# Two-layer FFN behind attention: order of a feature's attention steps and weight pieces in the first chunk

## The chip, the core and the metric

The kernel runs on one core of one Trainium2 chip. The metric is the time of the whole kernel on the device, in microseconds (us). A core has five engines that work side by side, each through its own queue and strictly in order: TensorE (PE, matrix products; PEld is its weight load), VectorE (DVE), ScalarE (ACT), GpSimd (POOL) and SyncE (SP, which issues the DMAs here). An instruction waits on semaphores for what it reads; what is queued behind it on its engine waits with it.

## What is computed

Sparse attention over 4 batches, 8 heads, 576 positions of 64 features, then two feed-forward layers on 2304 tokens. Cut to what matters here:

```python
def _attn_ref(q, k, v):                    # (4, 8, 576, 64)
    scores = np.matmul(q, k.transpose(0, 1, 3, 2)) / np.sqrt(D)
    # heads 0-3: the 32 positions up to the query; heads 4-7: earlier positions of equal pos % 32
    scores = np.where(masks, scores, -1e9)
    attn = np.exp(scores - scores.max(-1))
    attn = attn / (attn.sum(-1) + 1e-9)
    return np.matmul(attn, v)

def _moe_ref(x, w_in, w_out):              # (2304, 512) -> 2048 -> 512
    h = x @ w_in
    return (h - np.tanh(h)) @ w_out

def _moe2_ref(x, w_gate, w_val, w_out):    # 512 -> 1536 -> 512
    g = x @ w_gate
    return (g / (1 + np.exp(-g)) * (x @ w_val)) @ w_out
```

## The kernel before

Products of the layers are made in three matmuls each, with high and low parts of both factors (`mm3`, L188). So weights and activations have to be split first. The weights arrive as 64-bit words, and a piece of 128 x 512 of them goes through a chain of steps, the class `Piece` (L112): `high` and `low` on ACT (L124, L127), `clamp` and `shift` on DVE (L130, L134), `join` on POOL (L142), `sign` on DVE (L146), `head` on ACT (L152, the high part), `rest` on POOL (L155, the low part). Between the steps of a piece lie a few hundred nanoseconds to some microseconds, so `Feed.tick` (L178) interleaves three pieces: one tick loads a piece two ahead of its first use, does `high`, `low` of piece t, `clamp`, `shift`, `join` of piece t-1, and `sign`, `head`, `rest` of piece t-2.

The kernel has stages: attention of the first batch (with the first four pieces), the first layer in five chunks of up to 512 tokens (L1015), and the second layer. In a chunk, f runs over 16 blocks of 128 of the hidden features: `first_part` (L513, 12 matmuls of 512 columns into `ps_h`), `bend` (L518: tanh on ACT, L520, difference on DVE, L521), `parts` (L524: high part `gh` on ACT, L527, low part `gl` on DVE, L528), and one iteration later `second` (L531, 12 matmuls into the four banks `ps_acc`). Chunk 0 is the one in which the weights are still being prepared, two ticks per iteration: 32 pieces in all, of which 28 are made here; later chunks use them again.

Into the iterations of the first chunks the attention of the following batch is threaded, one `Group` (L252) of three query blocks of a pair of heads per iteration; in chunk 0 these are 12 groups, f = 0 to 11. A group's steps: `scores` (six matmuls, PE), `top` (masked scores and their minimum after a change of sign, three instructions on DVE, L273), `exp` (three on ACT with the row sums, L282), `norm` (a small step on ACT, L290, a reciprocal on DVE, L294, and the scaling of the three blocks on POOL, L296; this is called the normalisation), `turn` (three transposes on PE, L308), `bring` (copy to SBUF on DVE, L312), `value` (six matmuls, PE) and `keep` (copy on ACT, L330).

The order of instructions in each queue is the order of these calls, written out by hand (`tc.manual_schedule`). In chunk 0 one iteration f reads, before the change: normalisation of group f-1; `first_part` of f; `bend`; look-ahead loads; `value` and `keep` of group f-3; first tick; `scores` and `top` of group f; `second` of f-1; `turn` and `bring` of group f-1; `parts` of f; `exp` of group f; second tick. The buffers: `ps_h` has two banks, `ps_a`, which scores, transposes and values share, has two, `s` has three, the staged pieces five.

Of the kernel before, what the change touches and what calls it, by code (L numbers as in the profile page):

```python
# [13 lines left out]
AF = mybir.ActivationFunctionType  # L14
ALU = mybir.AluOpType
AX = mybir.AxisListType.X
# [27 lines left out]
KC = DM // P  # L44
# [29 lines left out]
def model_kernel(ctx: ExitStack, tc: tile.TileContext, q, k, v, mask, ident, sq, sk, sv, smask, w1, w2, out):  # L74
    nc = tc.nc
# [23 lines left out]
    def psum(pool, tag):  # L99
        return pool.tile([P, 512], F32, tag=tag, name=f"ps_{tag}")  # L100
# [94 lines left out]
    with tc.manual_schedule():  # L195
# [47 lines left out]
        def load_ahead(b, s):  # L243

            i, at = divmod(s, NGRP)
            if at == (-1 if b == 0 else 0) % NGRP and (i or b == 0):
                load_qk(b, i + 1 + (b == 0))
            i, at = divmod(s - 3, NGRP)
            if at == 0 and i > 0:
                load_v(b, i + 1)  # L250

        class Group:  # L252
# [25 lines left out]
            def exp(self):  # L278
                w = self.w
                self.sm = att.tile([P, 16], F32, tag="sm", name="sm", bufs=3)[:, :GB]  # L280
                for i in range(GB):
# [2 lines left out]
                        **({"accum_out": self.sm[:, i:i + 1]} if self.b else {}),  # L284
                    )

            def norm(self, eng):
                w = self.w
                if self.b:
                    nc.scalar.activation(self.sm, self.sm, AF.Copy, bias=1e-9)  # L290
                else:
                    nc.vector.tensor_reduce(out=self.sm, in_=self.s[:, :, :w], axis=AX, op=ALU.add)
                    nc.vector.tensor_scalar(self.sm, self.sm, 1e-9, None, ALU.add)
                nc.vector.reciprocal(self.sm, self.sm)  # L294
                if eng is nc.gpsimd:
                    nc.gpsimd.tensor_tensor(  # L296
                        out=self.s[:, :, :w], in0=self.s[:, :, :w], in1=self.sm.unsqueeze(2).to_broadcast([P, GB, w]),
                        op=ALU.mult,
                    )
                    return  # L300
                for i in range(GB):
                    s, r = self.s[:, i, :w], self.sm[:, i:i + 1]
                    nc.scalar.mul(s, s, r)
# [165 lines left out]
        def used(c, use):  # L469
            tag = f"w{slot_of(*use, c)}"  # L470
            if use in stream:
                c, i = divmod(c * NS + stream.index(use) + NSS, NS)
                if 0 < c < len(CHUNKS1):
                    fetching.append((c, i))
                    return
            if c >= len(CHUNKS1) - 1:
                slots.give((wpool, tag))
# [40 lines left out]
        def bend(ps, n):  # L518
            t = epool.tile([P, CHUNK], F32, tag="e", name="t")
            nc.scalar.activation(t[:, :n], ps[:, :n], AF.Tanh)  # L520
            nc.vector.tensor_tensor(out=ps[:, :n], in0=ps[:, :n], in1=t[:, :n], op=ALU.subtract)  # L521
            return ps

        def parts(t, n):  # L524
            gh = gpool.tile([P, CHUNK], F32R, tag="gh", name="gh")
            gl = gpool.tile([P, CHUNK], F32R, tag="gl", name="gl")
            nc.scalar.copy(gh[:, :n], t[:, :n])  # L527
            nc.vector.tensor_tensor(out=gl[:, :n], in0=t[:, :n], in1=gh[:, :n].bitcast(F32), op=ALU.subtract)  # L528
            return gh, gl

        def second(w, g, n, acc, start, stop):  # L531
            gh, gl = g
            for m in range(KC):
                mm3(acc[m][:, :n], w, m * P, gh[:, :n], gl[:, :n], start, stop)
# [480 lines left out]
        for c, (c0, n) in enumerate(CHUNKS1):  # L1015
# [9 lines left out]
            g = {}  # L1025
            for f in range(NF1):
                if f - 2 in gs and not strided and c > 0:
                    gs[f - 2].bring(nc.vector)
                if f - 1 in gs and not strided:
                    gs[f - 1].norm(nc.gpsimd)  # L1030
                restore()
                if strided:
                    if f == NF1 - 3 and b + 1 < B:
                        later = begin(b + 1)
                    if f == START[NGRP - 1] + 1:
                        load_qk(b, 3)
                    if f == START[NGRP - 1] + 4:
                        load_v(b, 3)
                if ahead:
                    ps = ahead.pop(0)  # L1040
                    first_part(ps, w1_t[f, 0], x, n, PAIRS[3:], False, True)
                else:
                    ps = psum(ps_h, "h")
                    first_part(ps, w1_t[f, 0], x, n, order, True, True)
                used(c, (f, 0))
                if c == last:
                    flow.run(KC * 3 * MM)
                    for eng in "AVAV":
                        flow.load(eng, 0.65)
                if c == 0 and f == 2:  # L1050
                    second(w1_t[0, 1], g.pop(0), n, acc, True, False)
                    gs[0].turn(ps_a, "a")
                t = bend(ps, n)
                if c == 0 and f == 2:
                    gs[0].bring(nc.vector)
                if c == 0:
                    load_ahead(b, f)
                if f - 3 in gs:
                    gs[f - 3].value(ps_a, "a")
                    gs[f - 3].keep()  # L1060
                if f - 2 in gs and strided:
                    gs[f - 2].bring(nc.scalar)
                if c == 0:
                    feed1.tick()
                if f in gs:
                    gs[f].scores(ps_a, "a")
                    gs[f].top()
                if f == (0 if c == 0 else 1):
                    acc = [psum(ps_acc, "acc") for _ in range(KC)]
                if c == 0 and f > 1:  # L1070
                    second(w1_t[f - 1, 1], g.pop(f - 1), n, acc, False, False)
                    used(c, (f - 1, 1))
                    if f - 1 in gs:
                        gs[f - 1].turn(ps_a, "a")
                        gs[f - 1].bring(nc.vector)
                g[f] = parts(t, n)
                if f == 0 and c > 0:
                    kept()
                if f in gs:
                    gs[f].exp()  # L1080
                if c == 0:
                    feed1.tick()
                if f > 0 and c > 0:
                    second(w1_t[f - 1, 1], g.pop(f - 1), n, acc, f == 1, False)
                    used(c, (f - 1, 1))
                    if c == last:
                        flow.run(KC * 3 * MM)
                if f - 1 in gs and c > 0:
                    gs[f - 1].turn(ps_a, "a")
                if strided:  # L1090
                    if f in gs:
                        gs[f].norm(nc.scalar)
                    strided.step(f)
                if strided and f == NF1 - 1:
                    for j in ((0, 4), (4, 8), (8, 9)):
                        strided.turn(*j, ps_a, "a")
# [362 lines left out]
```

## Time and profile before

| | |
|---|---|
| median of 3 runs | 921.43 us (920.67 to 923.9) |
| profiled execution, its own time | 920.19 us |
| its span, first to last instruction | 918.3 us |
| PE busy | 880.8 us (96%) |
| DVE busy | 644.5 us (70%) |
| ACT busy | 458.7 us (50%) |
| POOL busy | 337.5 us (37%) |
| mean granted clock of PE, share of 2.4 GHz | 0.994 |

The profile is that of one execution. Busy shares are over the whole span; chunk 0 of the first layer, which the change touches, lies between about 46 and 165 us. A wait is put down to the instruction that released it last. In a timeline a row's idle time, in brackets, is that of its own engine just before it; of the releaser named there, "POOL w L155" ahead of a POOL instruction means only that POOL was busy with that one before. Rows of one engine can overlap by some tens of nanoseconds, since an instruction starts while the one before drains.

### The profile page before, as it was taken

The numbers are of one execution on the slowest core, as the hardware profiler recorded it, in microseconds if no ns is written. First come the engines' busy times: TensorE is split into PE (matmuls) and PEld (weight loads), VectorE is DVE, ScalarE is ACT, GpSimd is POOL, SyncE is SP. The second block draws the span as 40 slices with busy tenths as digits, with TensorE's granted clock in tenths as the row PEclk, the third lists the DMA queues.
The fourth block names the chain that finished last, engine by engine and source line by source line (L and its number), as shares of the span: only waits on it lengthen the run. The fifth ranks groups of instructions, "written<-read, shape, count | busy, mean of one in ns | idle before, by whom it ended". The sixth has DMA issues, their size and how long they took to land. (4 is left out here: it accounts for less than half of the span.)

```text
span 918.3 us, 14160 instructions
## 1 busy us (share of the span) xinstructions
PE 880.8 (96%) x4918; PEld 722.3 (79%) x4918; DVE 644.5 (70%) x1222; ACT 458.7 (50%) x1034; POOL 337.5 (37%) x284
## 2 busy tenths in 40 slices
PE   8889998899999999999999988999999999999998
PEld 6567776777877778998887776888888887888888
DVE  6778786677776787326886785788877777966451
ACT  5577775534244523225555454555545446655431
POOL 2578887385526553001503421535544320000000
PEclk9899999999999999999999999999999999999999
DMA  8464743632343210426636642535452568968551
GB/s 272 154 195 155 255 158 113 241 110 82 103 140 118 69 46 24 146 85 237 221 92 205 207 149 82 183 117 165 154 184 87 200 216 291 344 229 278 198 202 42
DMA packets 66215, 150.38 MB, mean 164 GB/s; under 512 B 7200, under 2 KB 13344, under 8 KB 66144
## 3 DMA queue, kind: packets, MB, share of 16 engines
q1 hardware_dynamic: 65568, 149.04, 48.3%
q8 instruction: 39, 0.64, 0.3%
q10 hardware_dynamic: 576, 0.43, 0.2%
q14 instruction: 32, 0.26, 0.1%
HBM read 105.93 MB, written 43.52 MB: 163 GB/s over the span
## 5 line engine op out<-in xcount | busy, mean ns | idle before, releaser
L193 PE MATMUL ps_acc<-sl 128*128 128x512 f32 (+1 forms) x336 | 126.7, 377 | 5.0 <-DVE sl L738 5.0
L191 PE MATMUL ps_acc<-sl 128*128 128x512 f32 (+1 forms) x336 | 126.8, 377 | 3.4 <-ACT t L1206 3.4
L191 PE MATMUL ps_acc<-gl,w 128*128 128x512 f32 (+1 forms) x320 | 123.2, 385 | 3.4 <-DVE gl L528 3.3
L192 PE MATMUL ps_acc<-sl 128*128 128x512 f32 (+1 forms) x336 | 126.4, 376 | 0.0
L191 PE MATMUL ps_h<-xl,w 128*128 128x512 f32 (+1 forms) x320 | 121.1, 379 | 1.9 <-DVE gl L528 1.9
L193 PE MATMUL ps_h<-xh,w 128*128 128x512 f32 (+1 forms) x320 | 118.5, 370 | 0.7 <-POOL w L155 0.7
L193 PE MATMUL ps_acc<-gh,w 128*128 128x512 f32 (+1 forms) x320 | 118.5, 370 | 0.0
L192 PE MATMUL ps_acc<-gh,w 128*128 128x512 f32 (+1 forms) x320 | 118.3, 370 | 0.0
L192 PE MATMUL ps_h<-xh,w 128*128 128x512 f32 (+1 forms) x320 | 118.1, 369 | 0.0
L142 POOL TENSOR_TENSOR sl<-sl,st 128x512 int32<-128x512 int32 x36 | 52.0, 1450 | 164.6 <-DVE sl L134 134.2
L520 ACT ACTIVATE t<-ps_h 128x512 f32<-128x512 f32 (+1 forms) x80 | 44.0, 550 | 110.9 <-PE ps_h L193 110.9
L521 DVE TENSOR_TENSOR ps_h<-ps_h,t 128x512 f32<-128x512 f32 (+1 forms) x80 | 51.5, 643 | 65.5 <-ACT t L520 65.1
L976 DVE TENSOR_TENSOR sl<-sl 128x512 fp32r<-128x512 f32 (+1 forms) x120 | 73.9, 669 | 28.5 <-ACT sl L972 27.8
L528 DVE TENSOR_TENSOR gl<-ps_h,gh 128x512 fp32r<-128x512 f32 (+1 forms) x80 | 51.1, 638 | 39.5 <-ACT gh L527 38.0
L972 ACT CAST sl<-sl 128x512 fp32r<-128x512 f32 (+1 forms) x120 | 65.7, 599 | 25.2 <-DMA sl<-gd 19.0
L193 PEld LDWEIGHTS ps_acc<-sl 128*128 128x128 f32 x336 | 63.7, 190 | 17.2 <-DVE sl L738 5.9
L191 PEld LDWEIGHTS ps_acc<-sl 128*128 128x128 f32 x336 | 63.7, 190 | 16.8 <-ACT t L1206 5.5
L191 PEld LDWEIGHTS ps_acc<-gl,w 128*128 128x128 f32 x320 | 60.3, 188 | 18.5 <-DVE gl L528 6.0
L386 POOL TENSOR_TENSOR pr<-skv,sq 128x576 f32<-128x576 f32 (+8 forms) x40 | 56.3, 1437 | 50.2 <-DVE sc L393 30.6
L191 PE MATMUL ps_a<-sl 128*128 128x512 f32 (+1 forms) x192 | 70.3, 366 | 2.7 <-DVE t L1167 2.7
L192 PEld LDWEIGHTS ps_acc<-sl 128*128 128x128 f32 x336 | 63.6, 189 | 11.2
L193 PEld LDWEIGHTS ps_h<-xh,w 128*128 128x128 f32 x320 | 60.5, 189 | 11.8 <-POOL w L155 1.5
(125 smaller groups left out, 1960.9 us busy)
## 6 DMA issues: line engine op xcount, KB each, us to landing
st<-in_w SPq DMA_DIRECT2D x68, 512.0 KB, 4.7
gd<-t SPq DMA_DIRECT2D x84, 256.0 KB, 2.1
sl<-gd SPq DMA_DIRECT2D x84, 256.0 KB, 4.5
w<-w1s SPq DMA_DIRECT2D x32, 512.0 KB, 3.5
w3s<-sl SPq DMA_DIRECT2D x24, 256.0 KB, 4.0
sl<-w3s SPq DMA_DIRECT2D x24, 256.0 KB, 5.4
x2d<-o SPq DMA_DIRECT2D x18, 256.0 KB, 3.2
out_t<-t SPq DMA_DIRECT2D x18, 256.0 KB, 2.1
```

The source lines that it names most:

```text
L142: nc.gpsimd.tensor_tensor(out=mi, in0=mi, in1=self.lo, op=ALU.add)
L191: nc.tensor.matmul(ps, lhsT=wh, rhs=xl, start=start, stop=False, skip_group_check=goes_on)
L192: nc.tensor.matmul(ps, lhsT=wh, rhs=xh, start=False, stop=False, skip_group_check=goes_on)
L193: nc.tensor.matmul(ps, lhsT=wl, rhs=xh, start=False, stop=stop, skip_group_check=goes_on)
L386: nc.gpsimd.tensor_tensor(out=t, in0=x, in1=y, op=ALU.mult)
L520: nc.scalar.activation(t[:, :n], ps[:, :n], AF.Tanh)
L521: nc.vector.tensor_tensor(out=ps[:, :n], in0=ps[:, :n], in1=t[:, :n], op=ALU.subtract)
L528: nc.vector.tensor_tensor(out=gl[:, :n], in0=t[:, :n], in1=gh[:, :n].bitcast(F32), op=ALU.subtract)
L972: nc.scalar.copy(got[0][:, 0, :n], got[0][:, 1, :n].bitcast(F32))
L976: nc.vector.tensor_tensor(out=w[:, 1, :n], in0=w[:, 1, :n].bitcast(F32), in1=w[:, 0, :n].bitcast(F32), op=ALU.subtract)
```

## The change

In chunk 0 alone (c == 0) the iteration is written out anew. `norm` is cut into `least` (ACT), `invert` (DVE) and `scale` (POOL), so that they can stand apart. The new order of iteration f: `first_part`; (f = 2: `second` and `turn` of group 0 as before); `bend`; look-ahead loads; `value` and `keep` of f-3; `scores` and `top` of f; `parts` of f; `exp` and `least` of f; first tick; `second` of f-1, `turn` and `bring` of f-1; `invert` and `scale` of f; second tick. The number and the kind of instructions stay the same, and the chunks behind keep their order.

```diff
--- before.py
+++ after.py
@@ -284,14 +284,23 @@
                         **({"accum_out": self.sm[:, i:i + 1]} if self.b else {}),
                     )
 
+            def least(self):
+                nc.scalar.activation(self.sm, self.sm, AF.Copy, bias=1e-9)
+
+            def invert(self):
+                nc.vector.reciprocal(self.sm, self.sm)
+
             def norm(self, eng):
+                if self.b:
+                    self.least()
+                else:
+                    nc.vector.tensor_reduce(out=self.sm, in_=self.s[:, :, :self.w], axis=AX, op=ALU.add)
+                    nc.vector.tensor_scalar(self.sm, self.sm, 1e-9, None, ALU.add)
+                self.invert()
+                self.scale(eng)
+
+            def scale(self, eng):
                 w = self.w
-                if self.b:
-                    nc.scalar.activation(self.sm, self.sm, AF.Copy, bias=1e-9)
-                else:
-                    nc.vector.tensor_reduce(out=self.sm, in_=self.s[:, :, :w], axis=AX, op=ALU.add)
-                    nc.vector.tensor_scalar(self.sm, self.sm, 1e-9, None, ALU.add)
-                nc.vector.reciprocal(self.sm, self.sm)
                 if eng is nc.gpsimd:
                     nc.gpsimd.tensor_tensor(
                         out=self.s[:, :, :w], in0=self.s[:, :, :w], in1=self.sm.unsqueeze(2).to_broadcast([P, GB, w]),
@@ -1026,7 +1035,7 @@
             for f in range(NF1):
                 if f - 2 in gs and not strided and c > 0:
                     gs[f - 2].bring(nc.vector)
-                if f - 1 in gs and not strided:
+                if f - 1 in gs and not strided and c > 0:
                     gs[f - 1].norm(nc.gpsimd)
                 restore()
                 if strided:
@@ -1047,45 +1056,60 @@
                     flow.run(KC * 3 * MM)
                     for eng in "AVAV":
                         flow.load(eng, 0.65)
-                if c == 0 and f == 2:
-                    second(w1_t[0, 1], g.pop(0), n, acc, True, False)
-                    gs[0].turn(ps_a, "a")
+                if c == 0:
+                    if f == 0:
+                        acc = [psum(ps_acc, "acc") for _ in range(KC)]
+                    if f == 2:
+                        second(w1_t[0, 1], g.pop(0), n, acc, True, False)
+                        gs[0].turn(ps_a, "a")
+                    t = bend(ps, n)
+                    if f == 2:
+                        gs[0].bring(nc.vector)
+                    load_ahead(b, f)
+                    if f - 3 in gs:
+                        gs[f - 3].value(ps_a, "a")
+                        gs[f - 3].keep()
+                    if f in gs:
+                        gs[f].scores(ps_a, "a")
+                        gs[f].top()
+                    g[f] = parts(t, n)
+                    if f in gs:
+                        gs[f].exp()
+                        gs[f].least()
+                    feed1.tick()
+                    if f > 1:
+                        second(w1_t[f - 1, 1], g.pop(f - 1), n, acc, False, False)
+                        used(c, (f - 1, 1))
+                        if f - 1 in gs:
+                            gs[f - 1].turn(ps_a, "a")
+                            gs[f - 1].bring(nc.vector)
+                    if f in gs:
+                        gs[f].invert()
+                        gs[f].scale(nc.gpsimd)
+                    feed1.tick()
+                    continue
                 t = bend(ps, n)
-                if c == 0 and f == 2:
-                    gs[0].bring(nc.vector)
-                if c == 0:
-                    load_ahead(b, f)
                 if f - 3 in gs:
                     gs[f - 3].value(ps_a, "a")
                     gs[f - 3].keep()
                 if f - 2 in gs and strided:
                     gs[f - 2].bring(nc.scalar)
-                if c == 0:
-                    feed1.tick()
                 if f in gs:
                     gs[f].scores(ps_a, "a")
                     gs[f].top()
-                if f == (0 if c == 0 else 1):
+                if f == 1:
                     acc = [psum(ps_acc, "acc") for _ in range(KC)]
-                if c == 0 and f > 1:
-                    second(w1_t[f - 1, 1], g.pop(f - 1), n, acc, False, False)
-                    used(c, (f - 1, 1))
-                    if f - 1 in gs:
-                        gs[f - 1].turn(ps_a, "a")
-                        gs[f - 1].bring(nc.vector)
                 g[f] = parts(t, n)
-                if f == 0 and c > 0:
+                if f == 0:
                     kept()
                 if f in gs:
                     gs[f].exp()
-                if c == 0:
-                    feed1.tick()
-                if f > 0 and c > 0:
+                if f > 0:
                     second(w1_t[f - 1, 1], g.pop(f - 1), n, acc, f == 1, False)
                     used(c, (f - 1, 1))
                     if c == last:
                         flow.run(KC * 3 * MM)
-                if f - 1 in gs and c > 0:
+                if f - 1 in gs:
                     gs[f - 1].turn(ps_a, "a")
                 if strided:
                     if f in gs:
```

## Rows read from the trace of the kernel before

**Rows 1.** The page's list of engines: busy us, share of the span, instructions

```profile
PE 880.8 (96%) x4918; PEld 722.3 (79%) x4918; DVE 644.5 (70%) x1222; ACT 458.7 (50%) x1034; POOL 337.5 (37%) x284
```

**Rows 2.** PE's waits, 26 to 160 us: us in total, times, longest

```profile
PE ps_a L308 <- POOL s L296: 7.4, 11, 1.5
```

**Rows 3.** One iteration; busy (count) of PE, PEld, DVE, ACT, POOL; PEclk

```profile
81.80:89.60 7.80, 7.27 (x52) 5.48 (x51) 6.43 (x16) 5.83 (x18) 6.50 (x6) 1.00 0.41 134
```

**Rows 4.** Timeline of ACT, one iteration: start, duration, line, operation [idle before]

```profile
81.77 0.58 ACT L520 ACTIVATE t<-ps_h 128x512 f32<-128x512 f32 x1
...
85.18 0.62 ACT L152 CAST w<-m 128x512 fp32r<-128x512 f32 x1 [1.49 <-DVE m L146]
85.71 0.58 ACT L527 CAST gh<-ps_h 128x512 fp32r<-128x512 f32 x1
...
88.96 0.62 ACT L152 CAST w<-m 128x512 fp32r<-128x512 f32 x1 [0.48 <-DVE m L146]
...
89.59 0.58 ACT L520 ACTIVATE t<-ps_h 128x512 f32<-128x512 f32 x1
```

**Rows 5.** Timeline of DVE, the same iteration

```profile
81.90 0.17 DVE L294 RECIPROCAL sm<-sm 128x3 f32<-128x3 f32 x1 [0.79 <-ACT sm L290]
82.38 0.70 DVE L521 TENSOR_TENSOR ps_h<-ps_h,t 128x512 f32<-128x512 f32 x1 [0.31 <-ACT t L520]
82.99 0.83 DVE L130 TENSOR_SCALAR m<-m 128x512 f32<-128x512 f32 x1
83.86 0.69 DVE L134 TENSOR_SCALAR m<-m 128x512 int32<-128x512 int32 x1
84.47 0.68 DVE L146 SCALAR_TENSOR_TENSOR m<-st,m 128x512 int32<-128x512 int32 x1
...
85.55 0.54 DVE L312 COPY pt<-ps_a 80x384 f32<-80x384 f32 x1
86.32 0.69 DVE L528 TENSOR_TENSOR gl<-ps_h,gh 128x512 fp32r<-128x512 f32 x1 [0.22 <-ACT gh L527]
86.93 0.94 DVE L130 TENSOR_SCALAR m<-m 128x512 f32<-128x512 f32 x1
```

**Rows 6.** Timeline of POOL, the same iteration

```profile
82.23 1.30 POOL L155 TENSOR_TENSOR w<-m,w 128x512 fp32r<-128x512 f32 x1
83.50 0.77 POOL L296 TENSOR_TENSOR s<-s,sm 128x240 f32<-128x240 f32 x1
84.68 1.65 POOL L142 TENSOR_TENSOR m<-m,st 128x512 int32<-128x512 int32 x1 [0.42 <-POOL s L296]
86.28 1.30 POOL L155 TENSOR_TENSOR w<-m,w 128x512 fp32r<-128x512 f32 x1
```

**Rows 7.** Timeline of DVE, a stretch in which POOL is idle

```profile
49.66 0.42 DVE L130 TENSOR_SCALAR m<-m 128x512 f32<-128x512 f32 x1
50.11 0.43 DVE L134 TENSOR_SCALAR m<-m 128x512 int32<-128x512 int32 x1
```

**Rows 8.** Timeline of POOL near the chunk's end

```profile
156.87 1.27 POOL L155 TENSOR_TENSOR w<-m,w 128x512 fp32r<-128x512 f32 x1
```

**Rows 9.** Timeline of DVE at the same place

```profile
157.53 1.16 DVE L146 SCALAR_TENSOR_TENSOR m<-st,m 128x512 int32<-128x512 int32 x1
159.87 0.70 DVE L521 TENSOR_TENSOR ps_h<-ps_h,t 128x512 f32<-128x512 f32 x1 [1.18 <-ACT t L520]
```

**Rows 10.** Timeline of ACT, single rows of chunk 0

```profile
51.18 0.57 ACT L520 ACTIVATE t<-ps_h 128x512 f32<-128x512 f32 x1
...
58.30 0.58 ACT L520 ACTIVATE t<-ps_h 128x512 f32<-128x512 f32 x1
...
137.21 0.58 ACT L520 ACTIVATE t<-ps_h 128x512 f32<-128x512 f32 x1
...
159.25 0.59 ACT L520 ACTIVATE t<-ps_h 128x512 f32<-128x512 f32 x1
...
160.61 0.58 ACT L527 CAST gh<-ps_h 128x512 fp32r<-128x512 f32 x1 [0.77 <-DVE ps_h L521]
```

## The prediction

> **What bounds the kernel now.** I read the page's list of engines first: TensorE (PE) is busy 880.8 us of 918.3 [rows 1], so at first sight a microsecond that PE stops waiting is a microsecond off the time. Then the list of PE's waits in the stretch that the change touches, the first chunk of the first layer (46 to 165 us): 11 of its transposes wait for the normalisation on POOL, 7.4 us in all, 0.67 each [rows 2]. They are the waits that the change aims at. Third, one iteration of that chunk by engine: in 7.80 us PE is busy 7.27, DVE 6.43, ACT 5.83, POOL 6.50, at a granted clock of 1.00 (the 2.4 GHz level) [rows 3]. No engine but PE looks full. Last, the same iteration one engine at a time, and here the reading turns. Two tanh follow each other at 81.77 and 89.59 us [rows 4]. If PE set this distance, the tanh would wait for PE; ACT has no idle time before it, it has just come from the head of a weight piece at 88.96 (and a 0.1 us step). Going back from there, each step starts as the one before allows, between ACT and DVE alone: tanh 81.77, difference 82.38, clamp 82.99, shift 83.86, sign 84.47 [rows 5], head 85.18, high part 85.71 [rows 4], low part 86.32, clamp 86.93 [rows 5], a second shift and sign, head 88.96 [rows 4]. This loop is 7.82 us long and holds no PE. PE's 0.5 us of waiting in a period is what the loop leaves over, so the question is how long the loop is after the change.
>
> **What in the loop belongs to POOL.** The clamp of 82.99 takes 0.83 us and ends 0.29 after POOL's rest that ran from 82.23 for 1.30; the shift of 83.86 takes 0.69 and ends 0.28 after the normalisation (83.50, 0.77); the clamp of 86.93 takes 0.94 and ends 0.29 after the rest of 86.28 [rows 5, 6]. With POOL idle the same clamp takes 0.42 and the same shift 0.43 [rows 7]. So they wait for POOL's running instruction to end, and then need 0.28. Sign does so too: begun 0.66 after a rest that ran from 156.87 for 1.27, it took 1.16 and ended 0.55 after it [rows 8, 9]. In the other direction POOL waits for them: the join of 84.68 ends 1.18 after the sign that ended at 85.15, the normalisation 0.45 after the clamp that ended at 83.82 [rows 5, 6]. Steps that touch PSUM don't take part: the copy of 85.55 ran its 0.54 inside the join of 84.68, the low part its 0.69 inside the rest of 86.28, and neither did the reciprocal of 81.90 (0.17) [rows 5, 6].
>
> Who goes first when both wait is seen too: at 83.53 the clamp had waited and the normalisation was just ready; the clamp went first, then the normalisation, and the shift behind it [rows 5, 6]. They alternate, the one that was ready earlier first.
>
> **The change, step by step.** Nothing is computed less or more; only the order in the queues changes, in the 16 iterations of chunk 0. Removed from the head of an iteration: small ACT step, reciprocal and normalisation of the group before. Moved ahead of the first tick: scores, minimum, split, exponentials. Moved behind it: the reciprocal and the normalisation, now of this group. The two ticks, which stood half an iteration apart, now stand together with the transposed copy, the reciprocal and the normalisation between them. Queues passed: POOL's becomes join, rest, normalisation, join, rest; SP's keeps its order (look-ahead loads, then one load per tick), and its loads come two ticks ahead of use, as before; what they land in costs nothing while that holds.
>
> I walk one iteration with its tanh at 0. Difference 0.61 [rows 4, 5]. High part 0.74 behind it, 1.35 (159.87 to 160.61 [rows 9, 10]); the three minima, which ran between the sign's end at 85.15 and the copy at 85.55 [rows 5], fit in that gap. Low part 0.61 later, 1.96; first clamp 2.57 [rows 4, 5]. POOL is idle there (checked below), so clamp and shift end at 2.99 and 3.45 [rows 7], and the sign runs 3.36 to 4.05. The join, ready at 3.58, has to wait for that sign and ends 1.18 after it, at 5.23. ACT needs 2.77 from the start of the high part to the end of the exponentials and of the tick's first two steps (85.71 to 88.48, where its idle 0.48 begins [rows 4]), so with the small step its head starts at 4.2 and ends at 4.8, ahead of the join's end. DVE goes on with the copy (0.54, PE has long transposed) and the reciprocal (0.17) and reaches the second clamp near 4.6. The join runs: the clamp ends at 5.23 + 0.28 = 5.51. The rest, ready since 5.2, comes next: 5.51 + 1.17 = 6.68 (its 1.30 less the 0.13 that passes before it asks). The second shift: 6.96. The normalisation, waiting: 7.41. The second sign: 7.41 + 0.55 = 7.96. Its head starts 0.03 later and the next tanh 0.53 behind that (85.18 to 85.71 [rows 4]): 8.52. Join and rest end the list at 9.1 and 10.4, which is 1.9 in the next period, ahead of the clamp at 2.57: the pattern closes. **The period goes from 7.8 to 8.5.** What the old order had, a tick's clamp to sign beside idle POOL and its join and rest beside PSUM work of DVE, is given up in the second tick: there the loop runs through join, rest and normalisation one after the other.
>
> PE in that period: 7.27 us of work [rows 3] fit. Instead of 0.5 us PE now waits some 1.2 us per iteration, and I expect it ahead of the second product, for the rest of its weight piece, which ends at 6.7 where it ended near 5.8 (86.28 + 1.30, from the tanh of 81.77 [rows 4, 6]). The product is half of the large matmuls, under half of 7.27 us and more than a third, so the transpose behind it stands near 9.5, about 2 behind its normalisation: the 11 waits of [rows 2] vanish.
>
> The sum, iteration by iteration:
> - First one: ACT stands idle from the tanh's end (0.58) to 1.35, where the old order put two steps of a piece: +0.8.
> - Second one: 7.12 before (51.18 to 58.30 [rows 10]), where the queues were still half filled; full afterwards: 8.5, so +1.4.
> - Ten full ones: 78.91 before (58.30 to 137.21 [rows 10]). After: 85.2 plus some 0.5, as the last six groups are wider and the first has a copy more (the 0.5 is an estimate, a tenth of a normalisation's 0.77 six times): +6.8.
> - Three without attention: 22.04 before (137.21 to 159.25 [rows 10]). The walk without normalisation gives 8.07 twice; in the last, where the second tick has only its sign, 7.6: +1.7.
> - The last iteration has no tick; from its tanh on all stays as it was, and PE's wait for the last low part moves along.
>
> Together +10.7 us. The chunks behind are bound by PE with hardly a wait, and all their transfers are issued relative to this work, so nothing gives it back. The profiled execution took 920.19 (span 918.3): 930.9. The median is 921.43, 1.24 above it: 932.
>
> Bounds of what the rows don't show. The one grant that decides most is sign against normalisation after the second shift: the sign comes within 0.1 us of the shift's end, while the normalisation has waited. Should the sign win, the period is 8.52 − 0.45 = 8.07, ten times, and the sum 6.2. I take the other, by the row of 83.50 against 83.86, where the one ready earlier won. The Trainium skill has a rule on this: by "SBUF — State Buffer", section "SBUF: two separate sides", whichever of the two engines starts first gets the shared ports for its whole instruction and the other fully blocks. By it the normalisation wins and the sum is that of the walk; it does not say who is next when both wait, so it only lowers the chance of the other grant. Upwards: 0.3 us more per period, for semaphore delays in a chain that changes engine more often, gives +3.
>
> **Rivals.**
> (1) PE is the bound and the wait is simply removed: 7.4 us less [rows 2], 914. For it: 96% busy [rows 1]. It needs a loop under 7.27 us; without any waiting for POOL the walk would be 4.6 + 0.45 (49.66 to 50.11 [rows 7]) + 0.35 + 0.71 + 0.53, about 6.6. So it decides itself on whether the second tick's clamp, shift and sign wait together less than 0.6 us (and no slower than before up to 1.2); the walk has 1.9. Also if DVE kept the ports through all three, the loop would be under PE's 7.27 too. Against it: every contended row shown. The Trainium skill speaks for it: "Perfetto Trace Analysis", section "Identifying the Most-Contended Engine", says to optimise the engine with the highest occupancy first, and its next section to find the gaps on it and make what they wait for start sooner. By that the time would be 914. The trace disagrees in this stretch: ACT, at 5.83 of 7.80 us, has no idle time before the tanh.
> (2) The sign gets the ports ahead of the normalisation: +6.2, 927.6.
> (3) The delay is taken up at the chunk's end or by a transfer that was late anyway: no difference, 921.
>
> **How the numbers follow.** A comparison of this kernel can tell about 0.3% (2.8 us) from no change. The forecast has 0.76, (2) 0.11, both slower; (1) 0.08, faster; (3) 0.05. The range reaches from 926.5, one below (2), to 935.5, the forecast plus 3 and a little; (1) and (3) are left out, 0.13.
>
> **What would show it.** Right: no more waits of the transposes for the normalisation; 10 periods of 8.5 between tanh; second shifts of about 1.4 us and second signs of 1.1; new PE waits on the rest ahead of the second product. Shifts and signs that stay at 0.43 and 0.69 in the second tick prove the walk wrong, and then (1) holds. A period of 8.1 with signs of 0.7 is (2).

## The result

The changed kernel takes 935.21 us in the median, the kernel before 922.05 beside it: 1.0139 times as long (95% interval 1.0123 to 1.0156), 12.8 us more. One of its four executions took 1737.26 us; it counts in the median and not in the ratio, and nothing on record says why. The forecast was 932.0, in a range from 926.5 to 935.5. The profiled execution took 935.01 (span 933.1), 14.8 more than that of before.

The page of the changed kernel, its list of engines, beside [rows 1]:

```profile
PE 892.1 (96%) x4918; PEld 724.1 (78%) x4918; DVE 654.9 (70%) x1222; ACT 461.1 (49%) x1034; POOL 340.6 (36%) x284
```

The three largest of PE's waits in chunk 0 of the changed kernel (total us, times, longest), beside [rows 2]; its lines are nine higher behind `norm`, so 317 is the transpose, 305 the scaling, 339 `keep`:

```profile
PE ps_acc L193 <- POOL w L155: 8.8, 13, 1.1
PE ps_a L317 <- ACT x L339: 1.7, 8, 0.3
PE ps_acc L191 <- ACT w L152: 1.1, 2, 0.9
```

No transpose waits for the normalisation any more. The 7.4 us of [rows 2] are gone, and PE waits 8.8 us for the rest of weight pieces instead.

Why it waits, in one iteration. ACT of the changed kernel (start, duration, line, operation), beside [rows 4]:

```profile
86.52 0.59 ACT L529 ACTIVATE t<-ps_h 128x512 f32<-128x512 f32 x1
...
94.46 0.62 ACT L152 CAST w<-m 128x512 fp32r<-128x512 f32 x1 [1.95 <-DVE m L146]
94.99 0.59 ACT L529 ACTIVATE t<-ps_h 128x512 f32<-128x512 f32 x1
```

From tanh to tanh 8.47 us, where it was 7.82. ACT has now nothing to do for 1.95 us ahead of the second head; it waits for the sign on DVE. DVE in the same iteration, beside [rows 5]:

```profile
89.10 0.42 DVE L130 TENSOR_SCALAR m<-m 128x512 f32<-128x512 f32 x1
89.55 0.43 DVE L134 TENSOR_SCALAR m<-m 128x512 int32<-128x512 int32 x1
89.89 0.68 DVE L146 SCALAR_TENSOR_TENSOR m<-st,m 128x512 int32<-128x512 int32 x1
90.50 0.55 DVE L321 COPY pt<-ps_a 80x384 f32<-80x384 f32 x1
90.96 0.16 DVE L291 RECIPROCAL sm<-sm 128x3 f32<-128x3 f32 x1
91.05 0.97 DVE L130 TENSOR_SCALAR m<-m 128x512 f32<-128x512 f32 x1
92.05 1.39 DVE L134 TENSOR_SCALAR m<-m 128x512 int32<-128x512 int32 x1
93.36 1.07 DVE L146 SCALAR_TENSOR_TENSOR m<-st,m 128x512 int32<-128x512 int32 x1
```

and POOL, beside [rows 6]:

```profile
90.11 1.62 POOL L142 TENSOR_TENSOR m<-m,st 128x512 int32<-128x512 int32 x1 [1.75 <-issue]
91.70 1.46 POOL L155 TENSOR_TENSOR w<-m,w 128x512 fp32r<-128x512 f32 x1
93.12 0.77 POOL L305 TENSOR_TENSOR s<-s,sm 128x240 f32<-128x240 f32 x1
93.85 1.75 POOL L142 TENSOR_TENSOR m<-m,st 128x512 int32<-128x512 int32 x1
```

The first tick finds POOL idle: clamp 0.42, shift 0.43, sign 0.68, as in [rows 7]. The second runs against it: the clamp ends 0.29 us after the join (91.73), the shift 0.28 after the rest (93.16), the sign 0.54 after the normalisation (93.89). The three take 3.43 us, those of the first tick 1.53. The loop gets longer inside DVE rows that look like long instructions; a list of waits shows nothing of it.

The stretch from the first tanh of chunk 0 to the last is 112.42 us before (46.83 to 159.25 [rows 10]) and 123.07 after, 10.65 more. Single rows of ACT's timeline, first in the kernel before, then in the changed one:

```profile
46.83 0.59 ACT L520 ACTIVATE t<-ps_h 128x512 f32<-128x512 f32 x1
```

```profile
47.06 0.60 ACT L529 ACTIVATE t<-ps_h 128x512 f32<-128x512 f32 x1 [0.60 <-PE ps_h L193]
52.41 0.58 ACT L529 ACTIVATE t<-ps_h 128x512 f32<-128x512 f32 x1
60.86 0.59 ACT L529 ACTIVATE t<-ps_h 128x512 f32<-128x512 f32 x1
146.42 0.59 ACT L529 ACTIVATE t<-ps_h 128x512 f32<-128x512 f32 x1
170.13 0.59 ACT L529 ACTIVATE t<-ps_h 128x512 f32<-128x512 f32 x1
```

Of the profile's 14.8 us 0.2 lie ahead of this stretch and 3.9 behind it. Whether those 3.9 belong to the change is the question of the last experiment.

### The profile page after: what moved, and what is told of

Read it like the earlier page. It is cut to its first block, busy times and chain, and to the rows that moved or that the text cites. A ratio compares the mean times of both kernels' runs of the same rounds, so it can differ in the third digit from the quotient of the medians.

```text
span 933.1 us, 14160 instructions
## 1 busy us (share of the span) xinstructions
PE 892.1 (96%) x4918; PEld 724.1 (78%) x4918; DVE 654.9 (70%) x1222; ACT 461.1 (49%) x1034; POOL 340.6 (36%) x284
## 5 line engine op out<-in xcount | busy, mean ns | idle before, releaser
L193 PEld LDWEIGHTS ps_acc<-gh,w 128*128 128x128 f32 x320 | 60.6, 189 | 24.7 <-POOL w L155 14.4
L193 PEld LDWEIGHTS ps_acc<-sl 128*128 128x128 f32 x336 | 64.2, 191 | 17.7 <-DVE sl L747 6.3
L191 PEld LDWEIGHTS ps_acc<-sl 128*128 128x128 f32 x336 | 64.1, 191 | 17.3 <-ACT t L1230 6.0
L536 ACT CAST gh<-ps_h 128x512 fp32r<-128x512 f32 (+1 forms) x80 | 43.6, 544 | 60.1 <-DVE ps_h L530 60.1
```

The costliest lines, as they stand in the source:

```text
L191: nc.tensor.matmul(ps, lhsT=wh, rhs=xl, start=start, stop=False, skip_group_check=goes_on)
L193: nc.tensor.matmul(ps, lhsT=wl, rhs=xh, start=False, stop=stop, skip_group_check=goes_on)
```

## Experiments

Theory A is that of the prediction: DVE's clamp, shift and sign and POOL's instructions exclude each other, so chunk 0 is a loop through ACT, DVE and POOL, and its length depends on what POOL runs when these three steps come. Theory B: PE is the bound. Theory C: the cost comes from the steps moved ahead of the first tick. Each kernel's stretch from first to last tanh of chunk 0 is read from ACT's timeline of its profile and set against the 112.42 us of before; the whole time is compared with the kernel before, run beside it on the same chip. Each stretch is that of one execution; two profiles of the changed kernel differ by 0.4 us in it (123.07 and 122.66).

| kernel | chunk 0, first to last tanh | against 112.42 | usual period | whole time, ratio to before (95%) |
|---|---|---|---|---|
| before | 112.42 | | 7.79 to 7.91 | |
| changed | 123.07 | +10.65 | 8.47 to 8.59 | 1.0139 (1.0123 to 1.0156) |
| normalisation last | 118.50 | +6.1 | 8.10 to 8.11 | 1.0047 (1.0030 to 1.0063) |
| ticks apart | 116.31 | +3.9 | 8.01 to 8.16 | 1.0038 (1.0021 to 1.0056) |
| both of these | 112.77 | +0.35 | 7.80 to 7.90 | 0.9989 (0.9977 to 1.0002) |
| before, ticks together | 134.88 | +22.5 | 9.56 to 9.67 | 1.0239 (1.0214 to 1.0265) |
| before, transposes later | 113.53 | +1.1 | 7.83 to 7.95 | 1.0020 (1.0002 to 1.0037) |
| own order, scaling on POOL | 110.40 | -2.0 | 7.52 to 7.62 | 0.9964 (0.9947 to 0.9981) |
| own order, scaling on ACT | 111.55 | -0.9 | 7.25 to 7.31 | 1.0000 (0.9983 to 1.0016) |
| scaling on POOL, loads behind | 108.49 | -3.9 | 7.52 to 7.62 | 0.9968 (0.9951 to 0.9985) |
| scaling on ACT, loads behind | 108.46 | -4.0 | 7.25 to 7.33 | 0.9952 (0.9936 to 0.9968) |

The usual period leaves out one to three of the ten full periods in most kernels, also in the kernel before, which has one of 8.20. Where they bear on the argument they are named below.

### The normalisation behind the second tick

```diff
-                    if f in gs:
-                        gs[f].invert()
-                        gs[f].scale(nc.gpsimd)
                     feed1.tick()
+                    if f in gs:
+                        gs[f].invert()
+                        gs[f].scale(nc.gpsimd)
                     continue
```

> The changed kernel with one thing moved: reciprocal and normalisation stand behind the second tick, no longer between the two. Theory A (DVE's clamp, shift and sign and POOL's instructions exclude each other, and with the two ticks side by side the second one waits for join, rest and normalisation in turn): the second sign follows its shift at once and takes about 0.69, the period falls by one normalisation, from 8.5 to about 8.1 us, and the last tanh of chunk 0 comes 5 to 6.5 us later than in the kernel before instead of 10.9. The transposes wait for the normalisation again, and that costs nothing. Rival B (the stretch is bound by PE; what costs is who makes PE wait): the waits of the transposes are back, so the period is no shorter than 8.5. Rival C (the steps moved ahead of the first tick cost, the ticks don't matter): 8.5, no difference.

DVE's second tick in this kernel:

```profile
90.72 1.08 DVE L130 TENSOR_SCALAR m<-m 128x512 f32<-128x512 f32 x1
91.83 1.39 DVE L134 TENSOR_SCALAR m<-m 128x512 int32<-128x512 int32 x1
93.14 0.68 DVE L146 SCALAR_TENSOR_TENSOR m<-st,m 128x512 int32<-128x512 int32 x1
```

POOL's join and rest beside it:

```profile
89.87 1.64 POOL L142 TENSOR_TENSOR m<-m,st 128x512 int32<-128x512 int32 x1 [1.19 <-issue]
91.47 1.46 POOL L155 TENSOR_TENSOR w<-m,w 128x512 fp32r<-128x512 f32 x1
```

and the largest of PE's waits in chunk 0:

```profile
PE ps_a L317 <- POOL s L305: 8.4, 10, 1.4
```

The sign takes 0.68 again, clamp and shift still end 0.29 us after join and rest, and the period is 8.1: one normalisation of 0.45 less than the 8.52 of the walk. Ten transposes wait for the normalisation again, 8.4 us, more than the 7.4 of the kernel before, and the kernel is 0.9% faster than the changed one all the same. B and C fall here: the waits that the change took away are back and the time is shorter, and the early exponentials are still early.

### The first tick back in its place

```diff
                         gs[f - 3].keep()
+                    feed1.tick()
                     if f in gs:
                         gs[f].scores(ps_a, "a")
...
                         gs[f].least()
-                    feed1.tick()
```

> The changed kernel with one thing moved back: the first tick stands ahead of scores and minimum, half an iteration from the second; the normalisation stays ahead of the second tick. Theory A: the join and rest of the first tick run beside DVE's work on PSUM again; the second tick still has the normalisation in its way. Period about 8.05, in the three iterations without attention 7.5 as before, the last tanh 2 to 4 us later than before. Theory B: no transpose waits for the normalisation, so the time is 7 us under that of before, 914. Rival C: as the changed kernel, 8.5, since the steps moved ahead stay there.

No transpose waits for the normalisation here, as in the changed kernel, and yet it takes longer than the kernel before. DVE's second tick now:

```profile
89.76 0.40 DVE L130 TENSOR_SCALAR m<-m 128x512 f32<-128x512 f32 x1
90.19 0.69 DVE L134 TENSOR_SCALAR m<-m 128x512 int32<-128x512 int32 x1
90.80 0.68 DVE L146 SCALAR_TENSOR_TENSOR m<-st,m 128x512 int32<-128x512 int32 x1
```

Only the shift waits, for the normalisation, and ends 0.28 us after it:

```profile
89.99 0.61 POOL L305 TENSOR_TENSOR s<-s,sm 128x240 f32<-128x240 f32 x1 [0.37 <-DVE sm L291]
```

Four of the ten full periods are 8.01 to 8.04 and five, towards the wider groups, 8.15 or 8.16; one is 9.38, in which ACT waited 2.6 us for a weight piece to land. That is 1.2 us over its neighbours and belongs to no theory; such a wait stands in the kernel before as well, and comes up again below.

### Both together

> Both edits together: first tick back in its old place, reciprocal and normalisation behind the second tick. What is left of the change is that split and exponentials stand ahead of the second product. Theory A: period 7.8 and the time of the kernel before within 1 us in chunk 0. Rival C: 8.5 or thereabouts, since minimum, split and exponentials are still early.

112.77 us against 112.42, and a ratio whose interval holds 1: within that, the early split and exponentials are worth nothing and cost nothing. With the two kernels above this divides the loss of 10.65: the two ticks side by side with the normalisation last cost 5.7 (118.50 less 112.77), the normalisation ahead of the second tick alone 3.5 (116.31 less 112.77), both 10.3. Both kernels of the second difference have a late piece, with periods of 9.38 and 8.56, so about 0.5 of the 3.5 is not the order's. The two parts add up to 9.2; some 1 us comes only where both stand together.

### The kernel before with its ticks together

```diff
-                if c == 0:
-                    feed1.tick()
                 if f in gs:
                     gs[f].scores(ps_a, "a")
...
                 if c == 0:
                     feed1.tick()
+                    feed1.tick()
```

> The kernel before with one thing moved: the first tick stands directly ahead of the second, at the end of the iteration; the normalisation stays at the head of the next one. Theory A: this is the worst place, DVE's two ticks run against join, rest, join, rest and behind them the normalisation; working the queues through with the durations of the trace gives a period of 9.6 us and about 20 to 23 us in all. Theories B and C: at most some 2 us, since nothing but the weight pieces has moved, and those are used an iteration later.

22.5 us more in chunk 0, from moving steps that nobody needs before the next iteration. DVE's second tick in this kernel, and POOL at the same time:

```profile
98.86 1.52 DVE L130 TENSOR_SCALAR m<-m 128x512 f32<-128x512 f32 x1
100.42 1.39 DVE L134 TENSOR_SCALAR m<-m 128x512 int32<-128x512 int32 x1
101.73 0.68 DVE L146 SCALAR_TENSOR_TENSOR m<-st,m 128x512 int32<-128x512 int32 x1
```

```profile
98.48 1.62 POOL L142 TENSOR_TENSOR m<-m,st 128x512 int32<-128x512 int32 x1 [2.70 <-issue]
100.06 1.46 POOL L155 TENSOR_TENSOR w<-m,w 128x512 fp32r<-128x512 f32 x1
101.94 1.64 POOL L142 TENSOR_TENSOR m<-m,st 128x512 int32<-128x512 int32 x1 [0.42 <-POOL w L155]
```

The clamp ends 0.28 after the join of 98.48, the shift 0.29 after the rest of 100.06. POOL, which had to run its work in the same place, is idle 2.70 us ahead of it. This is the strongest point for A: the forecast of 20 to 23 was worked out from durations of the trace, and B and C had at most some 2.

### The kernel before without PE's wait

```diff
+                if c == 0 and f - 2 in gs:
+                    gs[f - 2].turn(ps_a, "a")
                 t = bend(ps, n)
-                if c == 0 and f == 2:
-                    gs[0].bring(nc.vector)
+                if c == 0 and f - 2 in gs:
+                    gs[f - 2].bring(nc.vector)
...
                     used(c, (f - 1, 1))
-                    if f - 1 in gs:
-                        gs[f - 1].turn(ps_a, "a")
-                        gs[f - 1].bring(nc.vector)
```

> The kernel before with one thing moved: the transposes of a group (and the copy behind them) stand 12 matmuls later in PE's queue, behind the next first product; the normalisation stays where it was. This takes the wait for the normalisation away from PE and leaves the order of the ticks alone. Theory B (PE is the bound, the 11 waits are worth their 7.4 us): the transposes no longer wait and the time falls by about 7 us. Theory A (the loop of ACT, DVE and POOL is the bound): the waits go all the same, but the time doesn't fall; the copy now stands between difference and clamp, so the period is 7.8 to 8.1 us and the time equal to 2.5 us longer.

PE's waits in chunk 0 of this kernel, the longest in total:

```profile
PE ps_a L265 <- ACT x L330: 8.5, 9, 3.4
```

The 11 waits for the normalisation are gone, and nine waits of the scores for a bank of `ps_a` have come, 8.5 us in all. The time did not fall by 7 us, it rose by 0.2%. By itself this does not decide between A and B, since PE's waits did not get less in all; it shows, as A has it, that PE's 0.5 us to spare in a period [rows 3] come back elsewhere when they are taken away in one place. One of the nine waits is 3.4 us long. In the iteration behind it PE ran partly at half clock (granted 0.81 in the mean from 68.23 to 77.01 us), that period took 8.78 us, and the tanh at its end waited 0.85 us for PE; this is most of the 1.1 us more in chunk 0.

### An order made from the theory

If A holds, an order can be worked out from the durations that keeps DVE's three steps clear of POOL's work. `at` is the number of the first tick; `step` does one step of the piece named, or nothing where it was made earlier:

```python
# scaling on ACT; f - 3, scores, minimum as before, then:
feed1.load(at + 3); feed1.do(at, "high", "low")
step(at - 1, "rebase"); step(at - 2, "sign")          # clamp, shift, sign
g[f] = parts(t, n)
gs[f].exp(); gs[f].least()
step(at - 1, "join"); step(at - 2, "head")
second(w1_t[f - 1, 1], ...); gs[f - 1].turn(ps_a, "a")
gs[f].invert(); gs[f].scale(nc.scalar)
step(at - 2, "rest")
step(at, "rebase"); step(at - 1, "sign"); step(at, "join")
feed1.load(at + 4); feed1.do(at + 1, "high", "low")
gs[f - 1].bring(nc.vector)
step(at - 1, "head"); step(at - 1, "rest")
```

The order with the scaling on POOL is, in the same words: first tick's `high`, `low`, `rebase`, `join`, `sign`; `value` and `keep`; scores and minimum; `parts`; `head`; `rebase` of the second tick; second product and transposes; `rest`; `high`, `low`, `join`, `sign` of the second tick; exponentials; `head`, `rest`; copy, reciprocal, scaling.

> An order of its own for chunk 0, made from theory A: every step of DVE that needs the port of POOL is put where POOL has just ended, with work of DVE on PSUM (minimum, low part, copy) between them; the exponentials stand behind the first half of the second tick, the normalisation on POOL last. Theory A, working the queues through with the durations of the trace: period 7.58, the three iterations without attention 7.24 each, 3 us less than before in all. Theory B: the normalisation is last in POOL's queue, so the transposes wait as before and nothing is gained.

> An order of its own for chunk 0 with the normalisation's scaling on ACT (three instructions of about 0.36 us) instead of POOL, which takes it off the port that DVE and POOL share. Theory A: the loop is then no longer than PE's own work, period 7.25 us, 4 to 5 us less than before. Rival: ACT has 5.8 us of work in a period and 1.1 more makes it the bound; then the period stays at 7.8 or above.

Most periods came out as worked out, 7.52 to 7.62 and 7.25 to 7.31; iteration 7 did not, with 9.49 in the one and 10.56 in the other. There, with the scaling on ACT:

```profile
103.02 0.66 ACT L124 ACTIVATE m<-st 128x512 f32<-128x512 f32 x1 [3.54 <-DMA st<-in_w]
```

So the theory of the loop held, and the sum did not (2.0 and 0.9 us less in chunk 0, where 3 and 4 to 5 were forecast in all): it had no term for a piece that lands late. Two more periods of the order with the scaling on ACT are long: the first, 7.70, whose cause was not followed up, and the one behind iteration 7, 8.31. In the last one PE had waited 3.30 us for a copy on DVE, late like the rest of that iteration, then ran partly at half clock (granted 0.79 in the mean from 109.25 to 117.56 us), and the tanh at its end waited 0.92 us for PE. SP's queue shows where the late piece comes from:

```profile
93.29 0.33 SPq L468 DMA_DIRECT2D w1s<-w  x1
93.67 0.42 SPq L231 DMA_DIRECT2D kt<-in_k  x1
94.14 0.78 SPq L232 DMA_DIRECT2D qt<-in_q  x1
94.98 0.48 SPq L240 DMA_DIRECT2D vt<-in_v  x1
95.58 2.91 SPq L118 DMA_DIRECT2D st<-in_w  x3
```

The piece is issued at 95.58, behind a store that waits for its rest and behind the loads of keys, queries and values, and lands 7.4 us later. The kernel before has the same order in SP's queue, and there ACT waits for the piece behind these loads too:

```profile
100.48 0.68 ACT L124 ACTIVATE m<-st 128x512 f32<-128x512 f32 x1 [2.28 <-DMA st<-in_w]
```

It was issued at 93.66 us and landed 6.7 us later, and this is the period of 8.20. In the slower loop of the changed kernel the piece is in time or nearly so: no such wait in its first profile, 0.5 us in its second.

### The look-ahead loads behind the pieces

```diff
                     t = bend(ps, n)
...
-                    load_ahead(b, f)
...
+                    load_ahead(b, f)
                     continue
```

> The order with the scaling on ACT, and one more edit: the look-ahead loads of keys, queries and values stand behind the iteration's two loads of weight pieces in SP's queue, no longer ahead of them. In the run without this edit the period was 7.26 us as worked out, but for one of 10.56 and one of 8.31, where ACT waited 3.5 us for a weight piece to land. Theory: the late piece was queued behind the three look-ahead loads (about 1 MB); with the edit that wait goes, all ten periods are about 7.3, and chunk 0 is 4 to 5 us shorter than before, the time near 918. Rival: the loads share the DMA engines and not the order is at fault, the piece lands as late as before and the time stays at 922.

> The same edit on the order with the scaling on POOL, where one period of ten was 9.50 for the same wait instead of 7.57. Theory: all ten periods about 7.6, chunk 0 some 3.5 to 4 us shorter than before, the time near 918.5. Rival: the late landing stays, and so does the time of 919.

SP's queue of the kernel with the scaling on ACT, and all that ACT waits for pieces in chunk 0:

```profile
91.93 0.33 SPq L468 DMA_DIRECT2D w1s<-w  x1
92.35 1.31 SPq L118 DMA_DIRECT2D st<-in_w  x2
93.75 0.47 SPq L231 DMA_DIRECT2D kt<-in_k  x1
```

```profile
ACT m L124 <- DMA st<-in_w: 0.4, 2, 0.3
```

The wait went from 3.7 us in this chunk to 0.4, and the kernel is faster than the one before and than the changed one: 0.9952 times the one before (0.9936 to 0.9968), where the changed one is at 1.0139. The first of its ten full periods is again 7.70, and one is still 8.26. PE, which had been busy for only 4.93 of the 7.60 us from 59.6 to 67.2, ran partly at half clock in it (0.79 granted in the mean from 67.3 to 75.5 us), and the tanh at its end waited 0.91 us for PE. At a period of 7.25 PE has next to nothing to spare: it is busy for 7.20 of the 7.20 us from 90.1 to 97.3.

```profile
67.30:75.50 8.20, 8.20 (x41) 6.30 (x43) 6.46 (x16) 6.68 (x20) 6.56 (x6) 0.79 0.43 142
```

With the scaling on POOL chunk 0 is 3.9 us shorter than before, as expected; the whole time, 0.9968, differs from that of the order without this edit (0.9964) by nothing that can be measured.

### What lies outside chunk 0

> The changed kernel itself, more often, beside the kernel before on one chip, for the part of its loss that lies outside chunk 0. Chunk 0 accounts for 10.7 us in the profile; the comparison gave 12.8 (11.3 to 14.4) and the profile 14.8, with two stretches of half clock in the second layer, behind waits of PE that the kernel before has as well. Theory: that rest comes and goes with the granted clock from run to run, as it does for the kernel before (its runs of higher mean clock are the shorter ones); then more runs bring the difference to 10.7 within 1.5, and the runs of one mean clock differ by about 10.7. Rival: the later start puts the second layer in a worse place for good, then the difference stays at 13 and the mean clock of the changed kernel is lower than that of the kernel before in the mean over the runs.

1.0113 (1.0085 to 1.0141): 10.4 us, with the 12.8 of the first comparison just inside the interval and the rival's 13 at its edge. Chunk 0 was 122.66 us in this profile, +10.2. Over the six executions of the changed kernel the mean granted clock goes from 0.988 to 0.994; the three at 0.988 took 934.69 to 937.45 us, the one at 0.994 930.48. Over the eleven of the kernel before it goes from 0.989 to 0.994; the three at 0.989 took 924.62 to 925.78, the one at 0.994 920.21. The relation is loose: the longest of the eleven, 926.36, had 0.991, and two at 0.993 differ by 2.5 us. At 0.994 the two kernels differ by 10.3 us, at 0.993 by 11.0 (933.54 against a mean of 922.5), at 0.992 by 11.9 (935.19 against a mean of 923.3). The place in the profile is the beginning of the second layer. The same 35 us in the changed kernel's first profile, in its second, and in that of before (the third number from the end of a line is PE's granted clock, ahead of DMA share and GB/s):

```profile
555.00:590.00 35.00, 29.93 (x111) 23.39 (x110) 20.38 (x32) 14.68 (x28) 7.63 (x7) 0.85 0.20 69
```

```profile
555.00:590.00 35.00, 29.99 (x117) 23.85 (x116) 21.86 (x35) 16.52 (x31) 6.80 (x7) 0.90 0.20 70
```

```profile
544.00:579.00 35.00, 29.98 (x124) 23.97 (x123) 23.34 (x35) 15.80 (x30) 10.44 (x9) 0.95 0.24 80
```

In both kernels PE waits there twice for the first combined operands, 5.0 us in total:

```profile
PE ps_acc L193 <- DVE sl L747: 5.0, 2, 3.0
```

Behind these waits the granted clock can fall to the 1.2 GHz level for some us. Read in stretches of 1 us, it did so behind the first wait only in the kernel before (about 550 to 553 us), and behind both in the two profiles of the changed kernel (562 to 565 and 576 to 582 in the first, 563 to 566 and 580 to 583 in the second). An estimate of the time lost, the missing share of the clock summed over these stretches, is 1.7 us before, 5.1 and 3.4 us after. From the last tanh of chunk 0 to the end of the span it is 763.0 us in the first profile of the changed kernel, 761.3 in its second and 759.1 in that of before. So 3.4 of the first profile's 3.9 us are this estimate's, and what remains is about half a microsecond in the last chunk of the first layer, near 430 us; the second profile has 1.3 us there, and the kernel of "Both together" 0.3, so that it is no clear mark of the change. It was not followed up.

In the profiles of the nine other kernels, with the same second layer, the same estimate gives between 0 and 3.4 us. So this part differs from one execution to the next whatever chunk 0 does. That the changed kernel is not a little worse off there in the mean is not shown: both of its profiles lie at the upper end or above, and its mean clock was 0.9905 against 0.9913, within what the executions scatter. The start differs too: the first tanh of chunk 0 comes at 47.06 us in the changed kernel's first profile and at 48.92 in its second, with no edit between them.

## Why the prediction was right

- The bound. "This loop is 7.82 us long and holds no PE" is shown three times: the normalisation put last brought the waits back and the kernel became faster than the changed one, the ticks put together at the end cost 22.5 us as the durations had it, and an order with a shorter loop and the same PE work is faster than the kernel before. The tanh did wait for PE in single iterations in which PE ran partly at half clock, 0.9 us each in the ones named above.
- The ports. The walk had the second tick's clamp end at 5.51, the shift at 6.96, the sign at 7.96, and the next tanh at 8.52 from the tanh. Measured from 86.52: 5.50, 6.92, 7.91, 8.47.
- The grant between sign and normalisation, which carried 4.5 us: the normalisation went first, at 93.12, and the sign of 93.36 took 1.07. Rival (2) is out; what it priced is the kernel with the normalisation last, which measured 6.1 in chunk 0 where the rival had 6.2.
- The terms of the sum: first iteration 0.8, measured 1.0 (5.35 against 4.35); second 1.4, measured 1.3 (8.45 against 7.12); the ten full ones 6.8, measured 6.65 (85.56 against 78.91); the three without attention 1.7, measured 1.7 (23.71 against 22.04). Together 10.7, measured 10.65; that they meet so closely is partly luck, since single terms are off by 0.1 to 0.2 both ways. The landing of pieces was put at nothing: the kernel before had lost some 0.3 us to a late one, in its period of 8.20, and the changed kernel is spared it.
- Rival (1) had the page's 96% and the wait list for it. The wait list was right about who waits for whom and said nothing about what a wait is worth.
- PE's new wait. The place was right in the main: the rest of the weight piece ahead of the second product (at its first low part). The list of waits shows 0.4 to 0.5 us per iteration with attention and about 1.0 in the last ones, and 0.2 ahead of the transposes, for `keep`, where 1.2 were forecast. But the list counts from the end of the matmul before, and matmul rows overlap: closely packed they start 0.23 us apart and last 0.39. The same iteration shows PE busy for 7.86 us, where [rows 3] had 7.27 for the same work, so 0.6 us of standing still hides in the busy time. Period less the 7.27 of [rows 3] is 1.2, as forecast.
- What was left out: the granted clock behind chunk 0. "Nothing gives it back" held, which also rules out rival (3): from the last tanh of chunk 0 on, the changed kernel took no less time than the one before. Nothing was said of what the second layer adds from one execution to the next, 3.9 us more than before in this profile, most of it by the clock. The range's upper end was 0.3 us per period for semaphore delays, a term that no run shows: the periods came out at 8.47 to 8.59, but for the first. The range held the result, 0.3 us under its upper end, because of a term that it did not contain; that was luck.

## What to carry to other kernels

Before a wait of the busiest engine is priced at its length, follow the chain back from an instruction that did not wait: if the loop closes without that engine, the wait is slack, and removing it only moves it. A busy share does not tell: PE was at 96% in the kernel before and in the changed one. Where two engines exclude each other, an instruction that waits for the other looks like a long one: compare the durations of one form with the other engine idle and busy, and lay the ends side by side. Then place such steps where the other engine is idle; moving independent preparation work by half an iteration cost 22 us here, and placing it well gained 4.

## What was not expected of the hardware

Two things outside the loop. The weight piece that stands behind three loads in SP's queue, together about 1 MB, landed 6.7 us after its issue in the kernel before and 7.4 in the order with the scaling on ACT; the median for such a piece of 512 KB in the kernel before is 4.7 us. The shorter the loop, the longer ACT waited for it: at most 0.5 us at periods of 8.1 and above, 2.3 to 2.6 at 7.8 to 8.05, 3.2 at 7.55 and 3.5 at 7.25. And the granted clock: executions of one and the same program differ by 6 us (920.21 to 926.36 for the kernel before), and those of the higher mean clock tend to be the shorter ones. That is half of what this change costs, and a comparison of one profile of each kernel would have put up to 3.9 us too much on the change.
